# Attention with beacon keys and a multiplicative FFN on one Trainium2 core: part of the first loads moves to the second DMA queue as fp32, and the first x is transposed on TensorE

## The chip, the cores and the metric

One core of one Trainium2 chip. The metric is device time in microseconds (us) of one execution of the program; lower is better. The profile shows one execution; times inside it count from its first instruction, and its span runs from the first to the last instruction.

## The reference

Shapes: B = 8 batches, H = 8 heads, S = 576 rows, 16 beacon rows, D = 64; x has 4608 rows of 512; w1, w2 are 512x1024, w3 is 1024x1024, w_out is 1024x512. All inputs and the output are fp32.

```python
k_all = np.concatenate([beacon_k, k], axis=2)          # 592 keys
v_all = np.concatenate([beacon_v, v], axis=2)
scores = scale * np.matmul(q, k_all.transpose(0, 1, 3, 2))
scores = np.where(causal, -1e9, scores)                # beacon keys always visible
a = np.exp(scores - scores.max(-1, keepdims=True))
a /= a.sum(-1, keepdims=True) + 1e-09
attn = np.matmul(a, v_all)                             # (B, H, S, D)
x = attn.transpose(0, 2, 1, 3).reshape(B * S, H * D)   # 4608 x 512
out = ((x @ w1) * (x @ w2) @ w3) @ w_out
```

## The kernel before

Everything is computed in fp16 with fp32 sums. The order of the instructions on each engine is the order in which the code is written; nothing is rescheduled.

**Attention.** A batch is eight steps: four pairs of heads, each in two halves of the query rows. Step `s` belongs to batch `b = s // 8`, with `r = s % 8`. `scores(s)` makes transposed scores on TensorE (L300), `exps` the exponentials on ScalarE (L309), `mask` the causal products on VectorE (L321), `values(s)` the product with v, with a column of ones in v for the sums (L338), then the division on VectorE (L346, L347) into `x16`, row-major. The scores of step `s + 1` are written ahead of the values of step `s`. Scores need q and k with the head dimension on the partitions (`qT`, `kT`): for batch 0 TensorE transposes them (L194), for later batches a DMA does (`transpose_qk`, L123 and L124, ten per batch). After the last pair of heads of a batch five more transposing DMAs (L358) bring `x16` into `xT`, the form that the FFN needs.

**FFN.** Since nothing stands between `@ w3` and `@ w_out`, the kernel multiplies the two first (`fuse`: TensorE transposes of w3, L203, and 64 matmuls, L213, into `Wt`). Then come nine chunks of 512 rows: `ff_ab` (64 matmuls, L233, with w1 and w2 in `w12`) and `ff_out` (32 matmuls, L254; the results leave by L265). All of this is one stream, 64 + 9 x 96 matmuls; `emit_ff(n)` writes its next n matmuls. The table `fill[s]` says how many go into step `s`, and `n_first` how many more between batch 0 and batch 1. In the kernel before that is 16 in each of steps 4 to 7, then 60, then 36 over batch 1, then some 11 in each step; what is left is written at the end. Chunk 1 needs rows of batch 1, chunk 2 of batch 2, and so on.

**Queues.** Two queues issue DMAs. POOL's loads everything that comes from memory and casts fp32 to fp16 on the way (q L99, k and v L108 with their beacon rows L112, w_out L172, w3 L176, w1 and w2 L179). SP's does the transposing DMAs and the output. Each queue issues in the order of the code, and an entry that waits holds up those behind it. On each queue at most eight DMAs are under way: an entry also waits for the landing of the one eight places ahead. q, k, v and their transposed forms have two buffers each (`b % 2`), so a load waits until the batch that last used its buffer is through with it.

Of the kernel before, what the change touches and what calls it, by code (L numbers as in the profile page):

```python
# [39 lines left out]
def kernel(  # L40
# [13 lines left out]
    nc = tc.nc  # L54
# [70 lines left out]


    for i in range(NB2):
        nc.vector.memset(k16s[i][64:128, 4, :], 0.0)
        nc.vector.memset(vas[i][64:128, 4, :, :], 0.0)
# [9 lines left out]
    load_q(0, 0)  # L139
    load_k(0, 0)  # L140
    load_q(0, 1)
# [8 lines left out]
    )  # L150
    load_k(0, 1)
    for c in range(2, NJT):
        load_q(0, c)
        load_k(0, c)
    for m, base in (
# [14 lines left out]
    for c in range(NJT):  # L170
        load_v(0, c)
    nc.gpsimd.dma_start(wo16, moe_w_out.rearrange("(t p) n -> p t n", p=P))  # L172

    w316 = xT[:, :, ds(M // 2, 2 * DF)].rearrange("p a (c r) -> p a c r", c=2)
    for kt in range(NFT):
        nc.gpsimd.dma_start(w316[:, kt // 2, kt % 2], moe_w3[ts(kt, P), :])  # L176
# [12 lines left out]

    for c in range(NJT):  # L190
        pt = psM.tile([P, 2, NT, P], FP16, name="pm")
        for i, d16 in enumerate((q16s[0], k16s[0])):
            for t in range(NT):
                nc.tensor.transpose(pt[:, i, t, :], d16[:, c, ts(t, P)], ident)  # L194
        nc.vector.tensor_copy(qTs[0][:, :, ts(c, P)], pt[:, 0])
        nc.scalar.copy(kTs[0][:, :, ts(c, P)], pt[:, 1])


# [126 lines left out]
    def values(s):  # L325
# [41 lines left out]
    for s in range(4, 8):  # L367
        fill[s] = 16
    for s in range(NSB, 2 * NSB):
        fill[s] = (96 - n_first) * (s - NSB + 1) // NSB - (96 - n_first) * (s - NSB) // NSB  # L370
    rest, n = 6 * 96 - LEFT, NS - 2 * NSB
    for s in range(2 * NSB, NS):
# [71 lines left out]
```

## Time and profile before

| | |
|---|---|
| median of 3 runs | 347.77 us (347.2 to 348.11) |
| the profiled execution | 346.73 us, span 345.0 us |
| mean granted TensorE clock | 0.951 |
| busy: TensorE, VectorE, ScalarE, POOL | 293.3, 152.5, 153.4, 121.7 us |
| first scores of batch 0, of batch 1 | 14.51, 76.87 us |

A timeline row reads: start, duration, engine, line, operation, output<-inputs, shape, count, and in brackets the idle time of that engine ahead of it and what ended it. A row of DMA issues gives the count, the size of one as written, and the median time from issue to landing. GB/s counts the bytes written; a load that casts reads twice as many.

### The profile page before, as it was taken

What the parts mean: (1) busy time and instruction counts of PE and PEld (TensorE: products, weight loads), DVE (VectorE), ACT (ScalarE), POOL (GpSimd) and SP (SyncE); (2) the same over time, 40 slices, a digit from 0 to 9 for tenths busy, and PEclk for the clock granted to TensorE, in tenths of its full rate; (3) what the DMA queues carried; (4) which work ended last, traced back from release to release, by engine and by line L of the source; (5) the groups of instructions that cost most, each with busy time, mean ns of one, the idle gap of its engine ahead of it and who ended that gap; (6) DMA issues with size and microseconds to landing.
All of it is one profiled execution on the core that took longest, in us unless ns stands there. A gap on an engine that the chain in (4) does not pass through costs nothing.

```text
span 345.0 us, 6756 instructions
## 1 busy us (share of the span) xinstructions
PE 293.3 (85%) x2696; PEld 149.0 (43%) x2696; DVE 152.5 (44%) x363; ACT 153.4 (44%) x214; POOL 121.7 (35%) x162
## 2 busy tenths in 40 slices
PE   2686980897943999599999989999999999999995
PEld 1353540344421445245554544555545544444442
DVE  3253430145611555426565546556555555344342
ACT  2481430237620675146636745664666473031220
POOL 8944558658419400950096048214000000000000
PEclk9998997699966899879999999999999999999999
DMA  9999999999999991999299999999833203301103
GB/s 66 119 159 209 196 170 139 150 155 154 172 162 156 142 141 29 145 202 148 42 121 213 141 116 164 189 137 144 198 79 73 111 2 67 125 1 61 63 0 122
DMA packets 182447, 42.99 MB, mean 125 GB/s; under 512 B 171664, under 2 KB 176784, under 8 KB 182416
## 3 DMA queue, kind: packets, MB, share of 16 engines
q0 software_dynamic: 121232, 19.67, 84.7%
q1 hardware_dynamic: 61184, 22.89, 38.3%
q8 instruction: 21, 0.34, 0.4%
q14 instruction: 10, 0.08, 0.1%
HBM read 39.32 MB, written 9.44 MB: 141 GB/s over the span
## 4 chain that ended last, share of the span: by engine, by line
PE 60%; DMA 23%; POOL 8%; ACT 3%; issue 2%; DVE 2%; SPq 2%; POOLq 0%; DVEq 0%
PE pm L233 28%; PE pm L254 13%; PE pv L338 8%; DMA xT<-x 6%; PE ps L300 5%; DMA k<-in_k_dram 5%; DMA qT<-q 5%; PE pm L213 4%; DMA xT<-in_moe_w_dram 3%; DMA q<-in_q_dram 3%; POOL q L99 2%; POOL va L108 2%; POOL k L108 2%; ACT pT L309 2%; SPq L358 1%
## 5 line engine op out<-in xcount | busy, mean ns | idle before, releaser
L233 PE MATMUL pm<-xT,w 128*128 128x512 f16 x576 | 136.8, 390 | 19.8 <-DMA xT<-x 19.8
L309 ACT ACTIVATE pT<-ps 128x736 f16<-128x736 f32 (+3 forms) x128 | 106.3, 863 | 43.2 <-PE ps L300 42.5
L244 ACT ACTIVATE a_sb<-pm 128x512 f32<-128x512 f32 x72 | 43.0, 597 | 109.0 <-PE pm L233 107.8
L233 PEld LDWEIGHTS <-w 128*128 128x128 f16 x576 | 55.2, 100 | 83.6 <-issue 27.2
L246 DVE TENSOR_TENSOR gT<-pm,a_sb 128x512 f16<-128x512 f32 x72 | 49.7, 690 | 67.5 <-PE pm L233 67.2
L254 PE MATMUL pm<-Wt,gT 128*128 128x512 f16 x288 | 67.8, 383 | 0.0
L108 POOL DMA_DIRECT2D va<-in_v_dram x40 | 33.7, 861 | 80.4 <-PE pv L338 57.4
L300 PE MATMUL ps<-qT,kT 64*128 64x80 f16 (+3 forms) x704 | 39.7, 237 | 13.4 <-ACT pT L309 6.4
L338 PE MATMUL pv<-va,pT 128*128 128x65 f16 x960 | 43.3, 198 | 2.7 <-DVE pT L321 2.6
L346 DVE RECIPROCAL rd<-pv 128x4 f32<-128x4 f32 x64 | 12.1, 189 | 74.3 <-PE pv L338 74.3
L338 PEld LDWEIGHTS <-pT 128*128 128x128 f16 x960 | 35.1, 100 | 13.2 <-issue 4.9
L300 PEld LDWEIGHTS <-kT 64*128 64x128 f16 x704 | 21.7, 97 | 43.7 <-issue 39.3
L254 PEld LDWEIGHTS <-gT 128*128 128x128 f16 x288 | 26.9, 98 | 29.6 <-issue 0.8
L99 POOL DMA_DIRECT2D q<-in_q_dram x40 | 34.7, 869 | 12.6 <-DMA k<-in_k_dram 3.3
L108 POOL DMA_DIRECT2D k<-in_k_dram x40 | 34.4, 859 | 9.1 <-DMA q<-in_q_dram 6.1
L264 DVE TENSOR_SCALAR ot<-pm 128x512 f32<-128x512 f32 x36 | 24.8, 690 | 21.5 <-PE pm L254 21.0
L347 DVE TENSOR_TENSOR x<-pv,rd 128x256 f16<-128x256 f32 x64 | 31.4, 491 | 2.6
L321 DVE TENSOR_TENSOR pT<-pT,MB 128x512 f16<-128x512 f16 x64 | 19.1, 325 | 1.6 <-ACT pT L309 1.6
L213 PE MATMUL pm<-wo,wT 128*128 128x512 f16 x64 | 15.7, 392 | 0.0
L321 DVE TENSOR_TENSOR pT<-pT,MA 128x480 f16<-128x480 f16 x32 | 12.8, 399 | 2.8 <-ACT pT L309 2.8
L222 ACT CAST Wt<-pm 128x512 f16<-128x512 f32 x8 | 4.7, 586 | 16.7 <-PE pm L213 16.7
L205 DVE COPY wT<-pm 128x1024 f16<-128x1024 f16 x8 | 5.5, 689 | 8.4 <-PE pm L203 8.4
(29 smaller groups left out, 56.9 us busy)
## 6 DMA issues: line engine op xcount, KB each, us to landing
out_dram<-ot SPq DMA_DIRECT2D x36, 256.0 KB, 3.0
q<-in_q_dram POOLq DMA_DIRECT2D x32, 128.0 KB, 9.7
k<-in_k_dram POOLq DMA_DIRECT2D x24, 128.0 KB, 10.8
va<-in_v_dram POOLq DMA_DIRECT2D x24, 128.0 KB, 6.4
xT<-in_moe_w_dram POOLq DMA_DIRECT2D x8, 256.0 KB, 13.0
w<-in_moe_w_dram POOLq DMA_DIRECT2D x8, 256.0 KB, 10.1
wo<-in_moe_w_out_dram POOLq DMA_DIRECT2D x1, 1024.0 KB, 10.8
k<-in_k_dram POOLq DMA_DIRECT2D x8, 112.0 KB, 8.4
```

Source lines behind the costliest of these rows:

```text
L99: nc.gpsimd.dma_start(q16s[b % NB2][:rows, c, :].rearrange("s (h d) -> s h d", h=H), q[b, :, ds(c * P, rows), :].rearrange("h s d -> s h d"),)
L108: nc.gpsimd.dma_start(dst[ds(p0, rows)], src[b, :, ds(s0, rows), :].rearrange("h s d -> s h d"))
L213: nc.tensor.matmul(pm, wT[:, rt, :], wo16[:, rt, :], start=(rt == 0), stop=(rt == NFT - 1),)
L233: nc.tensor.matmul(pm, w12[:, kt, ds(i * DF + kf * P, P)], xT[:, kt, ds(mc * 512, 512)], start=(kt == 0), stop=(kt == NKT - 1),)
L244: nc.scalar.activation(a_sb, pm, AF.Copy, scale=GS)
L246: nc.vector.tensor_tensor(gT[:, kf, :], pm, a_sb, ALU.mult)
L254: nc.tensor.matmul(pm, gT[:, kf, ts(mt, P)], Wt[:, kf, :], start=(kf == 0), stop=(kf == NFT - 1),)
L300: nc.tensor.matmul(ps[:, hh, ds(col, n)], kT[ds(hh * 64, 64), t, ts(jt, P)], qT[ds(hh * 64, 64), t, ds(q0, n)],)
L309: nc.scalar.activation(pT[:, :, ds(GO[g], GW[g])], pss[s][j][:, :, 0 : GW[g]], AF.Exp, scale=scale)
L321: nc.vector.tensor_tensor(blk, blk, m.unsqueeze(1).to_broadcast([P, 2, n]), ALU.mult)
L338: nc.tensor.matmul(pv[:, 2 * n + hh, 0:65], pT[:, hh, ds(col, P)], va[:, jt, 2 * t + hh, 0:65], start=(jn == 0), stop=(jn == len(BLK[i]) - 1),
L347: nc.vector.tensor_tensor(x16[:, ds(tiles[0], ni), ds(t * P, P)].rearrange("p i (h d) -> p i h d", h=2), pv[:, 0 : 2 * ni, 0:64].rearrange ...
```

## The change

- The five chunks of k of batch 0 (and its beacon rows) load as fp32 on SP's queue into a staging pool `stg` of six buffers; VectorE casts each into `k16` ahead of its transposes.
- w_out (four pieces) and w1, w2 (eight pieces of 128 rows) also load as fp32 on SP's queue, through the same six buffers. `cast_piece` casts a piece and issues the load of the next. One cast on VectorE stands in each of steps 0 to 6; the other five alternate between VectorE and ScalarE after the values of step 7.
- x of batch 0 is transposed by TensorE (20 transposes, with five copies from PSUM by VectorE and ScalarE) in the midst of `fuse`, eight matmuls after the values of step 7; the five transposing DMAs of batch 0 go away.
- `fill`: 5 matmuls in each of steps 3 to 7; `n_first` becomes 44 and counts from the end of `fuse`; 36 in batch 1 as before; 16 more than before are left for the end.
- The loads of q and k for batch `b + 2` are written in batch `b`, after the v of `b + 1`; those of batch 2 ahead of the loop.
- `ptp` (exponentials) has two buffers and not three.

```diff
-    ptp = ctx.enter_context(tc.tile_pool(name="ptp", bufs=3))
+    ptp = ctx.enter_context(tc.tile_pool(name="ptp", bufs=2))
+    stg = ctx.enter_context(tc.tile_pool(name="stg", bufs=6))
...
+    kst = []
+    for jt in range(NJT):
+        st = stg.tile([P, 2 * DM], FP32, name="st")
...
+        nc.sync.dma_start(
+            sv[ds(p0, rows)], k[0, :, ds(s0, rows), :].rearrange("h s d -> s h d")
+        )
+        if jt == 0:
+            nc.sync.dma_start(sv[0:Nb], beacon_k[0].rearrange("h n d -> n h d"))
+        kst.append((st, p0 + rows))
...
-    nc.gpsimd.dma_start(wo16, moe_w_out.rearrange("(t p) n -> p t n", p=P))
...
-    for c in range(4):
-        for i, w in enumerate((moe_w1, moe_w2)):
-            nc.gpsimd.dma_start(
-                w12[:, :, ds(i * DF + c * 256, 256)],
-                w[:, ts(c, 256)].rearrange("(t p) f -> p t f", p=P),
-            )
...
     for c in range(NJT):
+        st, rows = kst[c]
+        nc.vector.tensor_copy(k16s[0][:rows, c, :], st[:rows, 0:DM])
         pt = psM.tile([P, 2, NT, P], FP16, name="pm")
...
+    wo_v = moe_w_out.rearrange("(a c p) n -> a p c n", p=P, c=2)
+    pieces = [(wo16[:, ds(2 * a, 2), :], wo_v[a]) for a in range(4)]
+    for kt in range(NKT):
+        for i, w in enumerate((moe_w1, moe_w2)):
+            pieces.append((w12[:, kt, ds(i * DF, DF)], w[ts(kt, P), :]))
+    queued = []
+
+    def cast_piece(engine):
+        dst, st = queued.pop(0)
+        if engine is nc.scalar:
+            nc.scalar.copy(dst, st)
+        else:
+            nc.vector.tensor_copy(dst, st)
+        if pieces:
+            queued.append(staged(*pieces.pop(0)))
+
+    for _ in range(6):
+        queued.append(staged(*pieces.pop(0)))
+
+    def x0_transposed(i):
+        pt = psM.tile([P, NT, P], FP16, name="pm")
+        n = QTN[i]
+        for t in range(NT):
+            nc.tensor.transpose(pt[:, t, 0:n], x16s[0][:n, i, ts(t, P)], ident[:n, :n])
+        dst = xT[:, :, ds(QT0[i], n)]
+        if i % 2:
+            nc.scalar.copy(dst, pt[:, :, 0:n])
+        else:
+            nc.vector.tensor_copy(dst, pt[:, :, 0:n])
...
-        if t == NT - 1:
+        if t == NT - 1 and b > 0:
             for i in tiles:
                 nc.sync.dma_start_transpose(
...
-    LEFT = 40
-    n_first = 60
+    LEFT = 56
+    n_first = 44
+    n_second = 36
...
-    for s in range(4, 8):
-        fill[s] = 16
+    for s in range(3, 8):
+        fill[s] = 5
...
+    for c in range(NJT):
+        load_q(2, c)
+        load_k(2, c)
     for s in range(NS):
...
             values(s)
-            emit_ff(n_first)
+            emit_ff(8)
+            for i in range(NJT):
+                x0_transposed(i)
+            while queued:
+                cast_piece(nc.vector)
+                if queued:
+                    cast_piece(nc.scalar)
+                emit_ff(8)
+            emit_ff(64 + n_first - emitted)
...
+        if b == 0:
+            cast_piece(nc.vector)
...
             if r == 0:
                 for c in range(NJT):
-                    load_q(b + 1, c)
-                    load_k(b + 1, c)
-                for c in range(NJT):
                     load_v(b + 1, c)
+                for c in range(NJT if b + 2 < B else 0):
+                    load_q(b + 2, c)
+                    load_k(b + 2, c)
```

Here, with `staged`, a load on SP's queue is issued into a fresh `st` buffer.

On SP's queue, from the end of batch 0 on, there stood before (`xT` is x transposed, `qT_69` and `kT_71` the buffers of odd batches, `qT_68` and `kT_70` those of even ones, here batch 2; `out_dram<-ot` is an output):

```order
L358 DMA_TRANSPOSE xT<-x_267 128x4x128 x3
L358 DMA_TRANSPOSE xT<-x_267 128x4x80
L123 DMA_TRANSPOSE qT_69<-q_1_63 128x4x128
...
L123 DMA_TRANSPOSE qT_68<-q_0_62 128x4x128
L124 DMA_TRANSPOSE kT_70<-k_0_64 128x4x128
L265 DMA out_dram<-ot 128x512
...
L123 DMA_TRANSPOSE qT_68<-q_0_62 128x4x64
```

and stand now, on the same queue:

```order
L212 DMA st<-in_moe_w_dram 128x1024 x8
L124 DMA_TRANSPOSE qT_69<-q_1_63 128x4x128
...
L124 DMA_TRANSPOSE qT_68<-q_0_62 128x4x64
L125 DMA_TRANSPOSE kT_70<-k_0_64 128x4x128
L406 DMA_TRANSPOSE xT<-x_888 128x4x112
L406 DMA_TRANSPOSE xT<-x_888 128x4x128
L313 DMA out_dram<-ot 128x512
```

The x transposes of batch 0 left the queue, the weight pieces came ahead of it, and all ten transposes for batch 2 now stand ahead of the first output; before, eight of the ten stood behind it.

On POOL's queue, from the first v of batch 0 on (`va` holds v, `xT<-in_moe_w` is w3, which is parked in a part of `xT`, `w_59` is w1 and w2), there stood before, ahead of batch 1's q:

```order
L108 DMA va_66<-in_v_dram 80x8x64
L172 DMA wo_61<-in_moe_w_out_dram 128x8x512
L176 DMA xT<-in_moe_w_dram 128x1024 x8
L179 DMA w_59<-in_moe_w_dram 128x4x256 x8
L99 DMA q_1_63<-in_q_dram 128x8x64
```

and now:

```order
L100 DMA q_0_62<-in_q_dram 64x8x64
...
L109 DMA va_66<-in_v_dram 112x8x64
...
L109 DMA va_66<-in_v_dram 80x8x64
L188 DMA xT<-in_moe_w_dram 128x1024 x8
L100 DMA q_1_63<-in_q_dram 128x8x64
```

The k of batch 0, w_out, w1 and w2 are gone from between. From batch 1's q on, the order of POOL's queue is the same in both kernels: q and k of batch 2, then v of batch 2, then q and k of batch 3 follow one another as they did, since POOL ran ahead of the loop already.

On VectorE, around step 7 in the kernel now (`w_59<-st` is the cast of a piece of w1 or w2, `xT<-pm` the copy of a transposed x):

```order
L394 RECIPROCAL rd<-pv 128x6
L395 TENSOR_TENSOR x_294<-pv,rd 128x3x128
L253 COPY wT<-pm 128x1024
L244 COPY xT<-pm 128x4x112
L244 COPY xT<-pm 128x4x128
L244 COPY xT<-pm 128x4x80
L227 CAST w_59<-st 128x1024
```

None of these copies of x and none of the casts stood on VectorE before.

More of the change, by code (lines that the diff above doesn't have):

```diff
@@ L124, in transpose_qk @@
         nc.sync.dma_start_transpose(kTs[i][:, :, ds(c * P, P)], k16s[i][:, c, :])
+    kst = []
+    for jt in range(NJT):
+        st = stg.tile([P, 2 * DM], FP32, name="st")
+        p0 = Nb if jt == 0 else 0
+        s0 = max(0, jt * P - Nb)
+        rows = min(P - p0, S - s0)
+        sv = st[:, 0:DM].rearrange("s (h d) -> s h d", h=H)
+        nc.sync.dma_start(
[4 more added lines that the diff above has]
+        kst.append((st, p0 + rows))
     for i in range(NB2):
@@ L139 @@
     load_q(0, 0)
-    load_k(0, 0)
     load_q(0, 1)
@@ L150 @@
     )
-    load_k(0, 1)
     for c in range(2, NJT):
         load_q(0, c)
-        load_k(0, c)
     for m, base in (
@@ L196, with staged @@
         nc.scalar.copy(kTs[0][:, :, ts(c, P)], pt[:, 1])
+    def staged(dst, src):
+        st = stg.tile([P, 2 * DM], FP32, name="st")
+        if len(src.shape) == 3:
+            nc.sync.dma_start(st.rearrange("p (c n) -> p c n", c=2), src)
+            return dst, st.rearrange("p (c n) -> p c n", c=2)
+        nc.sync.dma_start(st, src)
+        return dst, st
+    wo_v = moe_w_out.rearrange("(a c p) n -> a p c n", p=P, c=2)
[24 more added lines that the diff above has]
+            nc.vector.tensor_copy(dst, pt[:, :, 0:n])
     def fuse():
@@ L363 @@
     NS = B * NSB
-    LEFT = 40
-    n_first = 60
+    LEFT = 56
+    n_first = 44
+    n_second = 36
     fill = [0] * NS
-    for s in range(4, 8):
-        fill[s] = 16
+    for s in range(3, 8):
+        fill[s] = 5
     for s in range(NSB, 2 * NSB):
-        fill[s] = (96 - n_first) * (s - NSB + 1) // NSB - (96 - n_first) * (s - NSB) // NSB
-    rest, n = 6 * 96 - LEFT, NS - 2 * NSB
+        fill[s] = n_second * (s - NSB + 1) // NSB - n_second * (s - NSB) // NSB
+    rest, n = 7 * 96 - n_first - n_second - LEFT, NS - 2 * NSB
     for s in range(2 * NSB, NS):
```

## The prediction

> **What bounds the kernel now.** I read the page first: engine sums, slices, sums of the DMA queues.
>
> ```profile
> span 345.0 us, 6756 instructions
> PE 293.3 (85%) x2696; PEld 149.0 (43%) x2696; DVE 152.5 (44%) x363; ACT 153.4 (44%) x214; POOL 121.7 (35%) x162
> PEclk9998997699966899879999999999999999999999
> DMA  9999999999999991999299999999833203301103
> ```
>
> TensorE is the bound, but not evenly: its granted clock (PEclk) sinks near slices 7, 11 to 13 and 17, all in the first half, and DMA is busy there. So I asked for windows between TensorE's stalls (columns: busy time and count of each engine, clock, DMA share, GB/s).
>
> ```profile
> 0.00:14.51 14.51, 5.60 (x40) 3.67 (x41) 4.18 (x22) 3.33 (x5) 13.34 (x24) 1.00 1.43 91
> 25.82:50.72 24.90, 21.94 (x205) 12.80 (x204) 8.78 (x19) 8.49 (x13) 13.10 (x17) 0.93 1.43 194
> 50.72:61.58 10.86, 0.00 (x1) 0.03 (x1) 0.75 (x2) 0.00 (x0) 9.07 (x12) 0.74 2.20 143
> 76.87:94.12 17.25, 15.22 (x216) 8.21 (x215) 9.66 (x29) 13.09 (x17) 11.57 (x15) 1.00 2.34 163
> 94.12:110.21 16.09, 5.45 (x57) 2.84 (x58) 3.26 (x9) 2.86 (x4) 8.17 (x11) 0.69 1.73 154
> 146.11:345.00 198.89, 189.91 (x1684) 94.08 (x1683) 98.70 (x219) 93.64 (x132) 37.22 (x47) 0.99 0.93 110
> ```
>
> After 146.11 TensorE is 95% busy: little is to be had there. Before it, the timeline of TensorE names the stalls, and the chain of waits gives the price of 64 matmuls undisturbed.
>
> ```profile
> 14.51 0.92 PE L300 MATMUL ps<-qT,kT 64*128 64x128 f16 x8
> 28.46 0.94 PE L203 MATMUL pm<-ident,xT 128*128 128x128 f16 x8 [2.64 <-DMA xT<-in_moe_w_dram]
> 30.54 2.62 PE L213 MATMUL pm<-wo,wT 128*128 128x512 f16 x8
> 33.01 0.61 PE L203 MATMUL pm<-ident,xT 128*128 128x128 f16 x8
> 33.45 1.89 PE L213 MATMUL pm<-wo,wT 128*128 128x512 f16 x8
> 61.58 15.36 PE L233 MATMUL pm<-xT,w 128*128 128x512 f16 x60 [10.86 <-DMA xT<-x]
> 76.87 0.55 PE L300 MATMUL ps<-qT,kT 64*128 64x128 f16 x8
> 96.86 0.49 PE L300 MATMUL ps<-qT,kT 64*128 64x128 f16 x4 [2.75 <-DMA kT<-k]
> 99.70 0.61 PE L300 MATMUL ps<-qT,kT 64*128 64x256 f16 x4 [2.35 <-DMA qT<-q]
> 100.24 1.50 PE L338 MATMUL pv<-va,pT 128*128 128x65 f16 x24
> 101.55 2.30 PE L254 MATMUL pm<-Wt,gT 128*128 128x512 f16 x5
> 110.21 4.14 PE L233 MATMUL pm<-xT,w 128*128 128x512 f16 x10 [4.90 <-DMA xT<-x]
> 146.11 1.87 PE L233 MATMUL pm<-xT,w 128*128 128x512 f16 x4 [4.03 <-DMA xT<-x]
> 150.06 3.24 PE L233 MATMUL pm<-xT,w 128*128 128x512 f16 x11
> 201.98 0.40 PE L300 MATMUL ps<-qT,kT 64*128 64x256 f16 x4 [1.58 <-DMA qT<-q]
> 202.31 0.90 PE L338 MATMUL pv<-va,pT 128*128 128x65 f16 x24
> 299.48 13.81 PE pm L233 x64
> ```
>
> The brackets are the idle time. After the longer ones the matmuls run slow at first: 10 in 4.14 us at 110.21, where 64 in 13.81 us makes 0.216 each. So a stall costs its length and a slow restart.
>
> **The change, front part (to the scores of batch 1, now at 76.87).** What DMA could do there:
>
> ```profile
> DMA packets 12474, 1.57 MB, mean 92 GB/s; under 512 B 12474, under 2 KB 12474, under 8 KB 12474
> DMA packets 6835, 3.95 MB, mean 198 GB/s; under 512 B 1977, under 2 KB 6072, under 8 KB 6834
> 16.34 0.96 POOL L172 DMA_DIRECT2D wo<-in_moe_w_out_dram  x1
> 17.20 3.84 POOL L176 DMA_DIRECT2D xT<-in_moe_w_dram  x7
> L108 POOL DMA_DIRECT2D k<-in_k_dram x40 | 34.4, 859 | 9.1 <-DMA q<-in_q_dram 6.1
> xT<-in_moe_w_dram POOLq DMA_DIRECT2D x8, 256.0 KB, 13.0
> q<-in_q_dram POOLq DMA_DIRECT2D x32, 128.0 KB, 9.7
> out_dram<-ot SPq DMA_DIRECT2D x36, 256.0 KB, 3.0
> ```
>
> The first two are the windows 0 to 17 and 28 to 48 us. In the first, DMA moved 92 GB/s, with POOL busy issuing (13.34 of 14.51 us); in the second, with large rows, 198. So the weights cannot go faster than they did from 28 on, but can begin sooner, beside the small rows.
>
> (a) *k of batch 0.* POOL loses five issues of 0.859 and the beacon rows, 4.8 us; q ends that much sooner, k comes beside it. A load with small rows and no cast on SP's queue is not shown; its bounds are the 3.0 us of an output and the 9.7 of a loaded q. I take scores at 10.5 instead of 14.51: -4.0. But v of batch 0, now issued from 7 us, shares the engines with pieces of w_out; later by 0 to 6.7 us (9.7 less 3.0). I take 2, nearer to the low end, for the pieces under way are at most six. Net -2.0. The casts of k lie ahead of the transposes on VectorE, which waits there for TensorE anyway.
>
> (b) *w3.* Its first issue moves from 17.20 to 12, with no w_out of 1 MB ahead of it, and is first needed near 21 (step 3). The wait of 2.64 goes, with its slow restart: 2.62 - 1.89 and about 0.94 - 0.61 twice, 1.4. Net -4.1; bounds -4.1 and 0, if the pieces on SP slow w3 to its old time. I take the first, since w3 gains 5 us and w1, w2 come after it.
>
> (c) *x of batch 0.* The idle 10.86 goes, and the slow restart, 15.36 - 60 x 0.216 = 2.4. Added: 20 transposes at 0.61/8, 1.5 us, and some 0.5 for the copies, which alternate on two engines; 39 matmuls of the fusion cover the rest, and the eight ahead of them cover the division of step 7. Net -11.3.
>
> (d) *Casts and smaller fills.*
>
> ```profile
> L205 DVE COPY wT<-pm 128x1024 f16<-128x1024 f16 x8 | 5.5, 689 | 8.4 <-PE pm L203 8.4
> L264 DVE TENSOR_SCALAR ot<-pm 128x512 f32<-128x512 f32 x36 | 24.8, 690 | 21.5 <-PE pm L254 21.0
> ```
>
> A cast of 1024 fp32 costs between 0.69 (1024 fp16) and 1.38 us (twice 512 fp32). Seven lie in steps 0 to 6. VectorE is busy 9.66 of 17.25 us over the eight steps of batch 1, so 1.2 a step, beside steps of 2.2 us; a cast fits where its piece has landed. Bounds 0 and 9.7 (all seven exposed); the cover is nearest to full, and I take 1.5 us. If a piece is late, VectorE holds the division behind it and TensorE with that: what is late next is the landing of pieces 6 to 11.
>
> (e) Sixteen matmuls fewer before batch 1 and more at the end: -3.45 at the mark, 0 in the sum. `ptp`: the buffer now reused belongs to values two steps back, done by then: 0.
>
> Sum: -2.0 - 4.1 - 11.3 + 1.5 = -15.9; scores of batch 1 at 76.87 - 15.9 - 3.45 = 57.5.
>
> **The change, after that.** (f) *Start of batch 2.* SP's queue:
>
> ```profile
> 72.05 1.20 SPq L124 DMA_TRANSPOSE kT<-k  x1
> 85.91 0.36 SPq L265 DMA_DIRECT2D out_dram<-ot  x1
> ```
>
> The last eight transposes for batch 2 stood 14 us behind an output that was not computed yet. By the new order all ten stand ahead of the first output, so they run before batch 1 ends: -2.75 - 2.35, and the restart (1.50 - 0.90; 2.30 - 5 x 0.216): -6.9. This comes from x leaving SP's queue and from the later `ff_out`, not from loading two batches ahead: on POOL's queue the loads stand in the order they had. I cost that edit at 0.
>
> (g) *Chunk 1.* Before, it began right at batch 2; now 16 matmuls of chunk 0 remain, so 21 matmuls (4.5 us) and the scores and values of two steps (0.55 and some 0.6 each) lie between the last values of batch 1 and it, 6.8 us.
>
> ```profile
> 103.91 6.17 DMA xT<-x
> ```
>
> This is the last x that it needs; it landed at 110.08, 8.3 us after those values ended (101.74). So 1.5 us of idling stay: -4.90 - (4.14 - 2.16) + 1.5 = -5.4; bounds -6.9 and 0.
>
> (h) *Chunk 2* comes 16 matmuls later too, over 10 us after its x: -4.03, restart 1.87 - 0.86 and 3.24 - 2.38, and 0.6 for the values between, as at 100.24: -6.5.
>
> (i) The 1.58 at 201.98 (transposes for batch 5 behind outputs) I leave: outputs come later against the batch, loads too.
>
> Sum: -15.9 - 6.9 - 5.4 - 6.5 = -34.7. The profiled execution took 346.73, so 312.0; it stands 1.04 under the median of the runs, 347.77. Forecast: 313.
>
> [...] DMA at 198 GB/s, written in halves, from 28 to 48 us shows the engines loaded without a second queue. [...]
>
> **Rivals.**
> 1. *DMA stays the bound of the front.* For: 198 GB/s does not rise with a second queue; small rows may starve beside large ones. Then w1, w2 land near 48 as now and q, k of batch 1 behind them; the scores of batch 1 begin near 70: 313 + 12 = 325.
> 2. *Slower.* The casts on VectorE, in order, pace batch 0 by the landing of pieces, in two rounds of six buffers. With the median landing of w3, 13.0, two rounds end near 35 us and hide. With (f) to (h) kept, it turns slower when the scores of batch 1 come after 76.87 - 3.45 + 18.8 = 92, which needs the last piece at about 72 (some 20 us of matmuls follow it), rounds of 33 us. At 36 a round: 353. Against: that median.
> 3. *POOL held up by the casts.* The pieces are the first copies from SBUF to SBUF on VectorE, and no row shows what POOL does beside one. The five of k, 3.5 us at 0.69, lie where POOL issues v; if they hold it, 313 + 3.5 = 316, and with half the pieces' 13.8 besides, 323. [...]
> 4. *The change does not do what it says at batch 2*: q and k of batch 2 land late behind v of batch 1 and the transposes still end after batch 1: 313 + 7 = 320.
> 5. *All is covered*: v not late, chunk 1 not late, casts hidden: 313 - 2 - 1.5 - 1.5 - 1.6 = 306.
>
> **How the numbers follow.** Forecast 0.60 (own range 307 to 320), rival 1 0.15, 2 0.04, 3 0.07, 4 0.07, 5 0.07. The range 305 to 326 takes in all but rival 2 and the tails. About 0.3% of the time, 1 us, can be told from no change. Only rival 2 is slower; same needs it halfway, 0.02; faster 0.94.
>
> **What the new profile would show.** Right: no wait of L281 for `xT<-x` at the first chunk; first scores near 10.5 and those of batch 1 near 57; more GB/s before 17 us; no wait of scores for `qT` or `kT` at batch 2; chunk 1 waiting under 2 us, chunk 2 none; clock 0.9 or more in every slice from 25 us on. Wrong: TensorE idle in steps 0 to 7 behind the division or the mask with VectorE waiting for `st`; L251 waiting for w3 longer than 3 us; scores of batch 1 waiting for transposes whose q landed late; POOL's issues of v longer than 0.86.

## The result: 328.37 us, faster, but by 19 us and not by 35

| | before | after |
|---|---|---|
| median | 347.49 us (346.31 to 348.11, 4 runs) | 328.37 us (327.29 to 328.72, 4 runs) |
| profiled execution, its span | 346.73, 345.0 us | 327.29, 325.6 us |
| first scores of batch 0, of batch 1 | 14.51, 76.87 us | 18.23, 65.94 us |
| last v of batch 0 landed | 19.5 us | 26.6 us |
| chunk 1, chunk 2 begin | 110.21, 146.11 us | 99.08, 131.21 us |

The ratio is 0.9448 [0.9414, 0.9483]. The forecast was 313 us, 305 to 326, so the direction was right and the size wrong, by 15 us. Of k_sp and k1_sp, below, the profiled execution was a slow one (331.54 and 341.08 us), so the times given for these two are medians of their three other runs.

The page of the changed kernel, the lines that answer to those shown of before:

```profile
span 325.6 us, 6823 instructions
PE 288.3 (89%) x2716; PEld 148.4 (46%) x2716; DVE 162.1 (50%) x381; ACT 156.1 (48%) x218; POOL 111.3 (34%) x147
PEclk9999999999997999999999999999999999999999
DMA  9999999999999999999999999997741221301103
```

The clock now sinks in one slice only, at 98.9 us (0.50 for 3.41 us). The first slices are not to be read, since the digit stands at 9 before the trace has a record of the clock: 14 matmuls of scores take 0.83 us at 27.29 and 0.52 at 34.90, and the trace's first record of the clock, at full, begins at 34.0 us (21.8 before). Stretches of the same work as before: up to the first scores, batch 1, batch 2 up to chunk 1, and from chunk 2 to the end (columns as in the prediction).

```profile
0.00:18.23 18.23, 5.11 (x40) 3.86 (x41) 6.19 (x27) 3.63 (x5) 11.67 (x22) 1.00 1.26 195
65.94:85.55 19.61, 15.21 (x216) 8.21 (x215) 9.60 (x29) 14.00 (x19) 13.64 (x17) 1.00 2.05 144
85.55:99.08 13.53, 8.45 (x107) 4.39 (x106) 6.27 (x16) 5.37 (x7) 6.29 (x8) 0.99 1.85 146
131.21:325.60 194.39, 185.65 (x1633) 91.62 (x1631) 98.44 (x217) 91.38 (x130) 36.64 (x46) 1.00 0.97 113
```

In the first row DMA moves 195 GB/s where it moved 91, and yet the stretch is 3.7 us longer. Batch 1 has the same 216 matmuls as before and takes 19.61 us where it took 17.25. TensorE's timeline names the waits:

```profile
17.26 0.61 PE L202 MATMUL pm<-ident,q 128*128 128x128 f16 x4 [2.27 <-DMA q<-in_q_dram]
18.23 0.91 PE L348 MATMUL ps<-qT,kT 64*128 64x128 f16 x8
23.85 0.32 PE L386 MATMUL pv<-va,pT 128*128 128x65 f16 x3 [2.30 <-DMA va<-in_beacon_v_dram]
25.57 1.79 PE L386 MATMUL pv<-va,pT 128*128 128x65 f16 x24
56.35 9.66 PE L281 MATMUL pm<-xT,w 128*128 128x512 f16 x44
65.94 0.55 PE L348 MATMUL ps<-qT,kT 64*128 64x128 f16 x8
74.22 0.35 PE L348 MATMUL ps<-qT,kT 64*128 64x80 f16 x10 [1.11 <-ACT pT L357]
89.78 0.35 PE L348 MATMUL ps<-qT,kT 64*128 64x80 f16 x10 [1.17 <-DMA kT<-k]
99.08 2.74 PE L281 MATMUL pm<-xT,w 128*128 128x512 f16 x6 [3.87 <-DMA xT<-x]
131.21 2.32 PE L281 MATMUL pm<-xT,w 128*128 128x512 f16 x10
```

Before chunk 0 (56.35) and chunk 2 (131.21) there is no wait any more, where there were 10.86 and 4.03. The 4.90 before chunk 1 became 3.87. Two waits are new, both for the small rows of batch 0: 2.27 for the last q and 2.30 for v. The values of step 1 begin at 25.57, where they began at 19.30:

```profile
19.30 1.50 PE L338 MATMUL pv<-va,pT 128*128 128x65 f16 x24
```

The window of 6 to 12.5 us of the DMA issues says why, first before, then after:

```profile
va<-in_v_dram POOLq DMA_DIRECT2D x1, 112.0 KB, 3.3
```

```profile
va<-in_v_dram POOLq DMA_DIRECT2D x3, 128.0 KB, 16.0
q<-in_q_dram POOLq DMA_DIRECT2D x1, 64.0 KB, 11.9
```

POOL issues v sooner than before (from 6.98 us on), but a v takes 16.0 us to land where the first took 3.3 (and the others up to 4.4). So the two halves of the miss are: the scores of batch 1 came at 65.94 and not at 57.5 (8.4 us), and from there to the end the kernel gained 8.5 us (268.1 to 259.7) where the forecast had 15.4 (6.9 us).

### The profile page after: what moved, and what is told of

The parts are those of the page before. It is cut to its first block, busy times and chain, and to the rows that moved or that the text cites. A ratio compares the mean times of both kernels' runs of the same rounds, so it can differ in the third digit from the quotient of the medians.

```text
span 325.6 us, 6823 instructions
## 1 busy us (share of the span) xinstructions
PE 288.3 (89%) x2716; PEld 148.4 (46%) x2716; DVE 162.1 (50%) x381; ACT 156.1 (48%) x218; POOL 111.3 (34%) x147
## 4 chain that ended last, share of the span: by engine, by line
PE 64%; DMA 15%; ACT 5%; POOL 4%; SPq 4%; DVE 3%; issue 3%; POOLq 0%; DVEq 0%
PE pm L281 27%; PE pm L302 16%; PE pv L386 9%; PE ps L348 6%; DMA va<-in_v_dram 5%; PE pm L261 4%; ACT pT L357 4%; DMA xT<-x 3%; DMA qT<-q 3%; DMA k<-in_k_dram 3%; DMA kT<-k 3%; POOL q L100 2%; SPq L125 2%; SPq L124 2%; PE pm L251 1%
## 5 line engine op out<-in xcount | busy, mean ns | idle before, releaser
L281 PE MATMUL pm<-xT,w 128*128 128x512 f16 x576 | 133.0, 382 | 3.9 <-DMA xT<-x 3.9
L281 PEld LDWEIGHTS <-w 128*128 128x128 f16 x576 | 54.0, 98 | 64.2 <-DMA xT<-x 4.4
L294 DVE TENSOR_TENSOR gT<-pm,a_sb 128x512 f16<-128x512 f32 x72 | 49.7, 690 | 48.4 <-PE pm L281 47.9
L302 PE MATMUL pm<-Wt,gT 128*128 128x512 f16 x288 | 66.7, 379 | 0.0
L348 PEld LDWEIGHTS <-kT 64*128 64x128 f16 x704 | 21.8, 97 | 42.2 <-issue 38.2
L109 POOL DMA_DIRECT2D k<-in_k_dram x35 | 29.9, 853 | 18.5 <-DMA va<-in_v_dram 7.0
L202 PE MATMUL pm<-ident,q 128*128 128x128 f16 x20 | 3.0, 308 | 13.1 <-DMA q<-in_q_dram 13.1
L204 ACT COPY kT<-pm 128x512 f16<-128x512 f16 x5 | 2.9, 586 | 14.4 <-DVE qT L203 14.4
```

Source lines behind the costliest of these rows:

```text
L109: nc.gpsimd.dma_start(dst[ds(p0, rows)], src[b, :, ds(s0, rows), :].rearrange("h s d -> s h d"))
L281: nc.tensor.matmul(pm, w12[:, kt, ds(i * DF + kf * P, P)], xT[:, kt, ds(mc * 512, 512)], start=(kt == 0), stop=(kt == NKT - 1),)
L294: nc.vector.tensor_tensor(gT[:, kf, :], pm, a_sb, ALU.mult)
L302: nc.tensor.matmul(pm, gT[:, kf, ts(mt, P)], Wt[:, kf, :], start=(kf == 0), stop=(kf == NFT - 1),)
L348: nc.tensor.matmul(ps[:, hh, ds(col, n)], kT[ds(hh * 64, 64), t, ts(jt, P)], qT[ds(hh * 64, 64), t, ds(q0, n)],)
```

## Experiments

All ratios are to the kernel before, run beside. "Mark" is the start of the scores of batch 1.

### One: is x on TensorE worth its price?

```diff
 # before.py
-        if t == NT - 1:
+        if t == NT - 1 and b > 0:
...
+            for i in range(NJT):
+                x0_transposed(i)
             emit_ff(n_first)
```

> The kernel before with one part of the change: x of batch 0 goes through TensorE (20 transposes after the values of step 7) instead of five transposing DMAs; loads and fills as before. Theory (the wait for the first x is worth its length and its restart, and the next thing in its place is the transposes of q and k for batch 1): the idle 10.9 us before the first chunk shrinks under 2 us, no slow restart, scores of batch 1 near 66 instead of 76.9, time 335 to 339. Rival (SP's queue or DMA throughput up to then sets the scores of batch 1 anyway): the scores of batch 1 wait for qT or kT and come at 72 or later, time 342 or more.

339.76 us, 0.9779 [0.9716, 0.9842], 0.8 us above the range that was expected. TensorE's timeline:

```profile
53.77 13.11 PE L233 MATMUL pm<-xT,w 128*128 128x512 f16 x60 [0.53 <-ACT xT L369]
70.70 0.35 PE L300 MATMUL ps<-qT,kT 64*128 64x80 f16 x10 [2.12 <-DMA kT<-k]
93.58 0.61 PE L300 MATMUL ps<-qT,kT 64*128 64x256 f16 x4 [5.07 <-DMA qT<-q]
104.94 4.31 PE L233 MATMUL pm<-xT,w 128*128 128x512 f16 x11 [5.72 <-DMA xT<-x]
```

The 10.86 became 0.53 and the mark came at 66.81, 10.1 us sooner. That is nearly the mark of the full change, which has 16 matmuls fewer ahead of it (3.45 us): with loads and queues as before, the front is 2.6 us shorter than in the full change. Then waits at batches 1 and 2 and at chunk 1 eat part of the gain.

### Two: small rows behind the weights (held_q, held_v, rows_1k)

Three variants of the changed kernel. held_q lets the first six weight pieces go only when the last q of batch 0 has been transposed; held_v only when v of batch 0 has landed (by a memset on POOL behind its eight loads of w3); rows_1k cuts the same pieces into rows of 1 KB.

```diff
 # held_q (held_v: nc.gpsimd.memset, behind the issues of w3, casts from step 2 on)
         st = stg.tile([P, 2 * DM], FP32, name="st")
+        nc.vector.memset(st[:, 0:1], 0.0)      # the first six pieces only
 # rows_1k
-    wo_v = moe_w_out.rearrange("(a c p) n -> a p c n", p=P, c=2)
+    wo_v = moe_w_out.rearrange("(a c p) n -> a p c n", p=P, c=4)
+    # pieces of 256 columns: four rows of 1 KB a partition, w1 and w2 likewise
```

> The changed kernel, but the first six weight pieces on SP's queue wait until the last q of batch 0 is transposed (a one-column memset on VectorE before each load). Theory (the DMA engines take rows from the two queues in turn, so each 256-byte row of q or v waits for a 2 or 4 KB row of a weight): the last q lands near 13.5 instead of 17.2 and the first scores come near 14.5 instead of 18.2; v, which still meets the pieces, lands its last near 24 instead of 26.6. Rival 1 (casts on VectorE hold up what POOL writes): the casts of k are still there, so q lands near 17 as now. Rival 2 (small rows are limited among themselves, weights do not matter): q as now, 17; v as now, 26. Time by the theory 325 to 328, by the rivals 328 to 331.

> The changed kernel, but the first six weight pieces on SP's queue wait until v of batch 0 has landed (memsets on POOL behind the w3 loads); the fusion begins in step 4 with 6 matmuls a step, and the casts in step 2. Theory (rows in turn): the last v lands near 18 instead of 26.6 and the values of step 1 come near 19.5 instead of 25.6, since nothing large is ahead of them; w_out then meets w3 and lands between 24 and 33, so VectorE may wait for pieces from step 2 on and the total moves by less than the 6 us won: 322 to 330. Rival 1 (casts hold POOL) and rival 2 (small rows limit one another): v lands after 23 as now. What each says of the values of step 1 decides, not the total.

> The changed kernel with the same bytes in the same twelve pieces, but each piece cut so that its rows are 1 KB instead of 2 or 4 KB (step 3 has 4 and step 4 has 6 matmuls of the fusion, since the pieces are cut by columns). Theory (rows in turn, one for one): a row of v waits for 1 KB instead of 2 or 4, so v lands sooner while the pieces are under way (last v near 23 to 24 instead of 26.6), and w3 on POOL's queue gains on w1 and w2 (last w3 under 40 instead of 43.5). Rival (the queues share by bytes): v and w3 land as now. Time by the theory 325 to 328, by the rival 328 or, if short rows cost the engines more, 330.

held_q: 331.14 us, 0.9503 [0.9434, 0.9572]. The last q landed at 14.2 us and not at 17.2, and the first scores came at 16.11, where 14.5 had been expected. v took 7.9 us (window 6 to 12.5) and the last had landed at 18.0 us and not at 26.6, since the held pieces were issued from 16.7 us on and met it little (24 had been expected); the values of step 1 began at 20.89 and not at 25.57.

```profile
va<-in_v_dram POOLq DMA_DIRECT2D x3, 128.0 KB, 7.9
```

The time did not fall, since VectorE then stood at a cast of w_out whose piece landed late, with a mask for TensorE behind it. Its row on VectorE, and TensorE's:

```profile
24.81 0.69 DVE L229 CAST wo<-st 128x1024 f16<-128x1024 f32 x1 [3.78 <-DMA st<-in_moe_w_out_dram]
26.57 0.51 PE L388 MATMUL pv<-va,pT 128*128 128x65 f16 x6 [3.41 <-DVE pT L371]
```

held_v: 333.55 us, 0.9597 [0.9522, 0.9672], in the same manner: last v at 18.3, values of step 1 at 21.1, then 6.5 us at 26.6 behind a cast. Both times lie above what was expected (325 to 328 and 322 to 330). Both show that the weight pieces are what held v up, and neither is a cure.

rows_1k: 331.76 us, 0.9551 [0.9493, 0.9608]. The last v landed at 28.5, no sooner than with larger rows, against the expectation of 23 to 24. The first six pieces are 1280 rows in the changed kernel and 3072 here, fewer than the 4736 of v, so the last of v comes behind all six either way: the sixth landed at 23.6 and 26.9 us. What the run shows is how two queues share. Rows by queue (q0 is POOL's, q1 SP's) in the stretch in which both have work, of rows_1k (16 to 24 us):

```profile
q1 hardware_dynamic: 1961, 1.94, 88.2%
q0 software_dynamic: 1960, 0.25, 46.8%
```

and of the changed kernel (12 to 20 us), whose pieces have mostly rows of 2 KB there:

```profile
q1 hardware_dynamic: 1509, 2.32, 91.1%
q0 software_dynamic: 1520, 0.19, 36.2%
```

In these stretches, where both queues have work and large rows stand in one of them, as many rows of the one passed as of the other, to within 1%, with rows of 1 KB and of 2 KB. Where both bring rows of 256 bytes the counts differ (4278 by POOL's and 3178 by SP's in the changed kernel, 4 to 12 us), and no run says why. Beside each row of v, 256 bytes in memory, went one of 1 or 2 KB, so while the weights moved 2.32 MB in the changed kernel, v and its kind moved 0.19. In what order the rows of the two queues follow one another, these counts do not show.

### Three: k of batch 0 alone on the second queue (x_fill, k_sp)

x_fill is x_only with the smaller fills of the change; k_sp is x_fill with k of batch 0 as fp32 on SP, and no weight there.

```diff
 # x_fill, on x_only
-    LEFT = 40
-    n_first = 60
+    LEFT = 56
+    n_first = 44
+    n_second = 36
 # k_sp, on x_fill
-    load_k(0, 0)                      # and the four others, POOL
+        nc.sync.dma_start(sv[ds(p0, rows)], k[0, ...])      # fp32, five chunks
+        nc.vector.tensor_copy(k16s[0][:rows, c, :], st[:rows, 0:DM])
```

> The kernel before with x of batch 0 on PE and with the smaller fills of the change (44, 36, 56); all loads stay on POOL's queue in their old order, no casts on VectorE. Theory 1 (the DMA engines were full before, row by row, so the second queue gains nothing): first scores 14.5, scores of batch 1 at 63.4 or up to 3 us later where they wait for the transposes of q and k (the last landed at 68.6 in the run with x alone), no wait before chunk 2, total 324 to 330, that is, no slower than the full change at 328.4. Rival (the loads on the second queue carry part of the gain): slower than the full change by 3 us or more, 331 to 336, with the w3 wait of 2.6 and a long wait for q and k of batch 1.

> As x_fill, and k of batch 0 alone goes as fp32 on SP's queue with five casts on VectorE; no weight does. This is term (a) of the prediction by itself. Theory 1 (small rows pass the engines at about 0.95 thousand a microsecond whatever queue brings them): the 9344 rows of q and k still take 10 us, first scores between 13 and 16, last v landed at 17 to 19, values of step 1 at 18 to 20.5, total within 2 us of x_fill. Rival (the prediction: POOL's issuing was the limit): first scores at 10.5, last v 4 to 5 us sooner than the 19.5 of before, total 3 to 4 us under x_fill.

x_fill: 331.39 us, 0.951 [0.945, 0.9571], first scores at 14.77; its time lies at the edge of what the rival had (331 to 336). k_sp: 328.19 us, 0.9425 [0.9347, 0.9504], first scores at 16.26. By the medians it is 3.2 us under x_fill, as its rival had it, but the intervals overlap, so whether k_sp is faster is open; that its first scores are not sooner is not. They came at 15.94, 15.93 and 16.20 in the three later kernels with the same front (qk1_pe, x1_pe, both_pe). Rows that started between 4 and 12 us, in before, x_fill, k_sp and after, a fence each:

```profile
DMA packets 7827, 0.98 MB, mean 123 GB/s; under 512 B 7827, under 2 KB 7827, under 8 KB 7827
```

```profile
DMA packets 7781, 0.98 MB, mean 122 GB/s; under 512 B 7781, under 2 KB 7781, under 8 KB 7781
```

```profile
DMA packets 7578, 1.34 MB, mean 168 GB/s; under 512 B 7578, under 2 KB 7578, under 8 KB 7578
```

```profile
DMA packets 7456, 1.34 MB, mean 168 GB/s; under 512 B 7455, under 2 KB 7455, under 8 KB 7456
```

One queue or two, it is 930 to 980 rows a microsecond. That is the mean of this stretch and not a ceiling; with v alone, from 14 to 16 us in k_sp, it is 1,200, and no run says why it is lower at first:

```profile
DMA packets 2410, 0.30 MB, mean 152 GB/s; under 512 B 2408, under 2 KB 2410, under 8 KB 2410
```

The GB/s of k_sp and of the changed kernel are higher only because an fp32 row is written with 256 bytes and a cast one with 128. q and k of batch 0 are 9344 rows (8 heads of 576 and 592), some 10 us at that rate, and the last of them landed at 14.2 us in x_fill and at 14.4 in k_sp. The rival, that POOL's issuing was the limit there, is out for the first scores. They come later than in x_fill, with the rows landed at the same time, because of the casts. VectorE in k_sp:

```profile
14.82 0.42 DVE L210 COPY qT<-pm 128x512 f16<-128x512 f16 x1 [1.53 <-PE pm L209]
15.16 0.51 DVE L205 CAST k<-st 80x512 f16<-80x512 f32 x1
```

The last k had landed at 14.16, but its cast stands behind the copy of a transposed q and begins at 15.16. The rival keeps a part behind the first scores: with five issues fewer on POOL, w_out landed at 24.0 us and not at 27.7, and the last w at 44.8 and not at 48.5.

### Four: the fills (old_fill) and the order of loads (q1_early)

old_fill is the full change with the fills of before from chunk 0 on; q1_early is x_fill with q and k of batch 1 ahead of the second half of w1 and w2 on POOL.

```diff
 # old_fill, on after.py
-    LEFT = 56
-    n_first = 44
+    LEFT = 40
+    n_first = 60
 # q1_early, on x_fill
+    load_w12(0); load_w12(1)
     for c in range(NJT):
         load_q(1, c)
         load_k(1, c)
+    load_w12(2); load_w12(3)
```

> The full change with the fills of before (60 matmuls of chunk 0 ahead of batch 1, 36 in its steps, 40 left): tests terms (e) and (g). Theory (the steps of batch 1 became long because 20 of their 36 fill matmuls are ff_ab, whose ScalarE scaling stands in one queue with the exponentials): batch 1 takes 17 to 17.5 us instead of 19.6 and its scores begin at 69.4; chunk 1 then begins right at batch 2 and waits for x 6 to 9 us instead of 3.87, and chunk 2 waits again; total 330 to 334. Rival (the length of batch 1 has nothing to do with which matmuls fill it): it still takes 19.3 us or more.

> As x_fill, and on POOL's queue q and k of batch 1 stand ahead of the second half of w1 and w2 (columns that the first 44 matmuls of chunk 0 do not read). Theory 1 (loads are bound by the engines, so the order on one queue decides): q of batch 1 lands about 5 us sooner (46 to 53.5 instead of 51 to 58.4), its transposes end by 64, scores of batch 1 at 63 to 64 with no wait for kT in its steps, total 318 to 324, faster than the full change. Rival (the transposes are late for another reason, their own length of some 1.3 us each in a row, or the second half of w1, w2 is now late): scores of batch 1 no sooner than 65.9, or a wait for w of 2 us and more in the steps of batch 1, total 326 or more.

old_fill: 340.15 us, 0.9769 [0.9717, 0.9822], worse than the 330 to 334 that were expected. TensorE's timeline, then SP's:

```profile
69.26 0.55 PE L348 MATMUL ps<-qT,kT 64*128 64x128 f16 x8
88.17 0.33 PE L348 MATMUL ps<-qT,kT 64*128 64x128 f16 x4 [1.67 <-DMA kT<-k]
93.94 0.61 PE L348 MATMUL ps<-qT,kT 64*128 64x256 f16 x4 [5.43 <-DMA qT<-q]
103.40 4.67 PE L281 MATMUL pm<-xT,w 128*128 128x512 f16 x11 [4.05 <-DMA xT<-x]
```

```profile
68.22 1.19 SPq L125 DMA_TRANSPOSE kT<-k  x1
78.29 0.36 SPq L313 DMA_DIRECT2D out_dram<-ot  x1
78.74 1.26 SPq L124 DMA_TRANSPOSE qT<-q  x1
```

Batch 1 lasts from 69.26 to 86.50, where the wait of 1.67 begins: 17.24 us, where before took 17.25, with four `ff_ab` matmuls among its 36. The full change, with twenty, takes 19.61. That the kind of matmul decides was as expected; that it does so by the scaling of `a_sb` on ScalarE, ahead of the exponentials for which TensorE waits 1.11 at 74.22, is the likeliest way, and no run separates it. Not expected was that the transposes for batch 2 stand again behind an output, from 68.22 to 78.74, and 5.43 us of TensorE with them.

So with the old fills the new loads gain nothing over x alone (340.15 against 339.76), and with the new fills 331.39 against 328.37, intervals overlapping. The fills are worth 8.4 us with the old loads and 11.8 with the new.

q1_early: 330.09 us, 0.9484 [0.9421, 0.9547], like x_fill and as the rival had it; 318 to 324 had been expected. q of batch 1 landed 5 us sooner (51.6 for the last) but its last transpose at 67.5 (70.6 in x_fill), and TensorE still waited 2.40 in batch 1. The ten transposes are what is slow, 17.6 us from the first landing to the last (13.7 in x_fill).

### Five: fewer DMA transposes (qk1_pe, x1_pe), and one more load on SP (k1_sp, all_three)

All on k_sp. qk1_pe transposes q and k of batch 1 on TensorE, x1_pe x of batch 1; k1_sp loads k of batch 1 as fp32 on SP too, once POOL has issued w3; all_three is all of it.

```diff
 # qk1_pe
-                transpose_qk(1, c)
+                qk1_transposed(c)                  # 8 transposes, copies by VectorE and ScalarE
+                emit_ff(8 if c < NJT - 1 else n_first - 40)
 # x1_pe
-        if t == NT - 1 and b > 0:
+        if t == NT - 1 and b > 1:
...
+        if s == 2 * NSB:
+            for i in range(NJT):
+                x_transposed(1, i)
 # k1_sp
-        load_k(1, c)
+        if b == 0 and r >= 2:
+            nc.vector.tensor_copy(k16s[1][:rows, r - 2, :], st[:rows])   # loaded by SP
```

> k_sp with q and k of batch 1 transposed on PE (40 transposes, eight ahead of each eight matmuls of chunk 0) instead of ten DMA transposes. Theory (what is left of the miss in batch 1 is that q and k pass the DMA engines twice, the second time at 1.3 us a transpose): added 40 x 0.61/8 = 3.1 us on PE; gone are the wait of 2.35 for kT and its slow restart of about 3; scores of batch 1 at 65, batch 1 takes 19.5 to 20 us instead of 24.1, batch 2 at 84.5 to 85.5 instead of 86.1; total 327 to 329. Rival (q and k themselves land too late, not the transposes): PE waits 2 us and more for q or k ahead of the transposes, total 330 or more.

> k_sp with x of batch 1 transposed on PE too, in the first step of batch 2. Term (g) by itself: before chunk 1 PE waits 4.49 for the DMA transpose of x and restarts slowly for 3.4 us at half the clock (about 1.7 lost). Theory: both go, 20 transposes of 1.5 us and their copies come instead, total 4 to 5 us under k_sp, 324 to 325.5. Rival (the wait only moves: q and k of batch 2 or 3, or chunk 2's x, are late next): total within 2 us of k_sp's 329.

> k_sp with k of batch 1 also as fp32 on SP, issued when POOL has issued w3 (20 us), so beside w_out and w3; five casts in steps 2 to 6. Theory 1 (rows take turns on engines that are full): w_out, w3 and the last w land 2 to 4 us later than the 24.0, 34.1 and 44.8 of k_sp, q of batch 1 lands about as then (53.8 at the last, or 1 to 3 us sooner), total 327 to 331. Rival (POOL's issuing, 0.86 us a load, is the limit): q of batch 1 lands by 49.5, its transposes 4 us sooner, no wait for kT in batch 1, total 325 or less.

> qk1_pe, k1_sp and x1_pe together on k_sp. If the three remove waits that follow one another, 320 to 324, faster than the full change (328.4); if PE then waits for q and k of batch 2, whose DMA transposes landed at 84.9, or the loads of batch 2 and 3 set the pace, 325 to 329.

qk1_pe: 325.91 us, 0.9395 [0.9326, 0.9464]: scores of batch 1 at 62.12 and of batch 2 at 81.92, no wait for kT. x1_pe: 325.47 us, 0.936 [0.9303, 0.9416]: chunk 1 without a wait at 96.50, chunk 2 at 127.88. Both as expected or a little better.

k1_sp: 337.00 us, 0.9701 [0.9617, 0.9785], and all_three 338.09, 0.9728 [0.9674, 0.9782]: both far worse than either theory. VectorE and TensorE in k1_sp:

```profile
37.07 0.43 DVE L441 CAST k<-st 128x512 f16<-128x512 f32 x1 [11.80 <-DMA st<-in_beacon_k_dram]
38.56 0.51 PE L359 MATMUL pv<-va,pT 128*128 128x65 f16 x6 [11.23 <-DVE pT L342]
```

The small rows of k, now on SP, were issued from 25.0 us on and so beside POOL's w3, w1 and w2; they took 11.4 to 18.8 us to land. The cast for them stood on VectorE ahead of a mask, and TensorE lost 11.23 us (10.95 in all_three). Here the small rows were SP's and the larger ones POOL's, and it was the small ones again that came late, with as many rows of each: from 29 to 37 us of k1_sp, 1304 by POOL and 1307 of k by SP. The stall itself is rival 2 of the prediction, casts that pace batch 0 by late landings, in another kernel.

### Six: do the staged weights carry a gain of their own? (after_x1, both_pe)

after_x1 is the full change with x of batch 1 on TensorE, as in x1_pe; both_pe is qk1_pe and x1_pe together, so it has no weight on SP.

> The full change with x of batch 1 transposed on PE too: term (g) on the changed kernel itself. In it PE waits 3.87 for the DMA transpose of x before chunk 1 and then runs at half the clock for 3.4 us (1.7 lost). Theory: both go for 20 transposes (1.5 us) that the copies delay little, and the queue of DMA transposes of batch 2 and 3 is five shorter: 3 to 5 us under 328.4, 323.5 to 325.5. Rival (in the changed kernel the wait only moves to q and k of the next batches): 327 or more.

> k_sp (k of batch 0 on SP, every other load by POOL, no weight staged) with q and k of batch 1 and x of batch 1 transposed on PE. Theory (the weights' second queue and their casts bring nothing that the engines had free, so a version without them is at least as fast once the DMA transposes are out): scores of batch 1 at 62, batch 2 at 82, no wait before chunk 1, total 320 to 323.5, below after_x1. Rival (the staged weights carry a gain of their own): 325 or more, above after_x1.

after_x1: 329.29 us, 0.9486 [0.9449, 0.9523], no faster than the full change. both_pe: 322.80 us (321.79 to 326.01), 0.9306 [0.9269, 0.9343]: faster than the full change and than after_x1 beside it, with w_out, w1 and w2 loaded as before. Its time is as expected, its scores of batches 1 and 2 (64.23 and 84.03) came 2 us later than that. It is the fastest median here, though the interval overlaps that of x1_pe. Rows of TensorE's timeline, and windows of 3.41 us (as long as the clock stayed at 0.50 in after_x1), the first of the two in each kernel with the wait at batch 4 in it, of after_x1:

```profile
146.56 0.61 PE L348 MATMUL ps<-qT,kT 64*128 64x256 f16 x4 [2.29 <-DMA qT<-q]
142.95:146.37 3.42, 1.32 (x9) 0.41 (x7) 0.91 (x3) 2.00 (x3) 0.00 (x0) 1.00 1.69 133
146.37:149.78 3.41, 3.22 (x32) 2.02 (x33) 1.10 (x3) 0.00 (x0) 0.88 (x2) 0.50 0.66 107
```

and of both_pe, with its line of the granted clock:

```profile
95.05 1.46 PE L248 MATMUL pm<-xT,w 128*128 128x512 f16 x6
145.07 0.40 PE L315 MATMUL ps<-qT,kT 64*128 64x256 f16 x4 [2.71 <-DMA qT<-q]
140.66:144.08 3.42, 1.70 (x11) 0.58 (x9) 1.27 (x3) 2.00 (x3) 0.00 (x0) 1.00 1.69 154
144.08:147.49 3.41, 2.42 (x35) 1.53 (x36) 1.12 (x3) 0.07 (x1) 0.89 (x2) 1.00 1.11 139
PEclk9999999999999999999999999999999999999999
```

In after_x1 the 3.87 went and chunk 2 began at 127.58, 3.6 us sooner than in the full change; then waits of 2.29 at 146.56 and 1.82 at 207.37, each with 3.4 us at half the clock behind it, gave it back. So the rival was right for this kernel: the wait moved. In both_pe a longer wait, 2.71, cost no clock.

## Why the prediction was wrong

**The step that failed is the first reading.** From 92 GB/s up to 17 us against 198 later, the prediction concluded that the weights "can begin sooner, beside the small rows". GB/s was the wrong column: the line of DMA's busy share quoted ahead of it read 9 from the first slices on, and with 128 bytes written a row 978 rows a microsecond are 123 GB/s (the 92 have the idle first microseconds in them). That a second queue found no room is shown by what happened: it brought no more rows a microsecond (947 and 932), and the weights beside v delayed it by 7 us, which holding them back undid. This step carries 8.4 of the 15.4 us; the rest is in (e), (f) and (g). The prediction took POOL's issuing (13.34 of the first 14.51 us) for time that fewer issues would save; in k_sp five issues fewer brought the last q and k no sooner (14.4 us, 14.2 in x_fill), so most of that time was hidden behind the rows.

**(a)** k of batch 0: forecast -4.0 and v +2. k alone on SP gave first scores 1 to 1.5 us later (14.77 to 15.93 or 16.26): the casts of k on VectorE, put at nothing in the prediction, cost that. The weights behind it on the same queue moved v by 7 us (19.5 to 26.6). What they did to the first scores differs between executions: 18.23 in the changed kernel, 16.38 in old_fill with the same instructions up to there; the last v landed at 26.7 in old_fill too, and the values of step 1 began there at 25.69. At the values of step 1 the net is +6.3, not -2.0: the 8.3 us between these are the miss of the front. The bound for v, 0 to 6.7, came from 9.7, the median of q loads, none of which had weights on the other queue beside it; v's 16.0 lies outside it.

**(b)** The wait for w3 went, but not because w3 came sooner: its first piece landed at 27.8 us (28.4 before). The step that needs it came later. In k_sp, without weights beside it, the piece landed at 25.3.

**(c)** x on TensorE: forecast -11.3, x_only -10.1 at the mark. Right to 1.2 us.

**(d)** Casts: from the values of step 1 to the mark 40.4 us; before it was 57.6, and the forecast's terms (b), (c), (d) and (e) make 40.2 of that; the cover held. A cast of 1024 took 0.69 us, the lower bound. That the sums agree so closely is luck in part, since TensorE's matmuls were slow for longer than before (the 0.83 us at 27.29 against 0.52 at 34.90, with the first record of full clock at 34.0 us and not at 21.8), which the forecast did not have. The cover is thin: when pieces land later, TensorE waits 3.41 (held_q), 6.5 (held_v) and 11.23 us (k1_sp, where the pieces are k).

**(e)** "Sixteen matmuls fewer: 0 in the sum" left out that twenty of the 36 in batch 1 become `ff_ab`. Batch 1 lengthened by 2.36 us, and old_fill shows it at 17.24 with four.

**(f)** The two waits at batch 2, 5.10, became one of 1.17. Mechanism right, but x leaving SP's queue does not do it: old_fill, where it has left too, waits 1.67 and 5.43. The later `ff_out` is needed; no run has it without the other.

**(g)** Chunk 1: 3.87 left and not 1.5, since the last x that it needs landed 11.8 us after the values of batch 1 ended (87.27 to 99.03) and not 8.3, the landing time of before; and the slow restart stayed (six matmuls in 2.74 us, 1.4 more than at 0.216). (e), (f) and (g) miss 2.36 + 1.17 + 2.37 + 1.4 = 7.3 us; the second half of the miss is 6.9.

**(h), (i)** Chunk 2 without a wait, as forecast; the late wait for qT is 1.19 (1.58 before).

**The edit to two batches ahead** was costed at 0. No run tests it alone; the order of POOL's queue from batch 1 on is the same either way.

**The rivals.** Rival 1 is what happened, "small rows may starve beside large ones", with 325 as its time, and the last of w1 and w2 did land near 48 "as now" (47.2, and 48.4 before); it put the delay on q and k of batch 1, and it fell on q and v of batch 0. Its time is near by luck: its mark was 70, and the rest of the miss is (e) to (g). That "198 GB/s does not rise with a second queue" did not hold as written (28 to 40 us: 204 before, 284 after), but as read it did: 4.86 MB before (2.43 written, all cast) and 4.87 after (1.49 written with a cast by POOL, and 1.89 by SP as they were). Rival 4 came in part (1.17 of 5.10). Rival 3 came on a small scale: POOL issues a v in 862 ns on average, where it took 861 before; but two issues that a cast of a piece met took 1.20 us (37.90) and 1.24 (49.06), where the longest of a q, k or v took 1.02 before, and a cast that met an issue took 1.09 us (28.42) instead of 0.69. Not each meeting did this: the issue at 40.28 took 0.94 and the cast at 30.45 took 0.69. Together that is about 1 us. Rivals 2 and 5 did not come here. Of the signs named for "right", first scores at 10.5, the mark at 57, no wait for `kT` at batch 2, chunk 1 under 2 us and the clock in every slice failed; more GB/s before 17 us came true and meant nothing.

What stays open is how much the staged weights cost or gain by themselves with the new fills: x_fill and the full change differ by 3.0 us with overlapping intervals. That they are not needed, both_pe shows.

## What to carry to other kernels

Whether DMA has room is read from rows per microsecond and the busy share, not from GB/s: rows of 256 bytes kept the engines at a busy share of 9 with little over half the bytes of large ones (123 GB/s written against 198). A second queue brought no more rows there (7578 in 8 us by both, 7827 by one), and beside larger rows the small ones passed one for one (1520 to 1509), so what is needed first is better kept clear of larger rows: the last v landed at 18.0 us in held_q and at 26.6 in the changed kernel. A cast that stands ahead of other work on an engine makes all of it wait for the load: 11.80 us of VectorE and, behind it, 11.23 of TensorE in k1_sp. Before a gain is summed from waits that follow one another, ask of each what will be late next: here it was fifteen transposes by DMA, and without them k_sp's 328.19 us became 322.80.

## What was not expected of the hardware

- The row rate hardly changed with the queue or with the cast: from 4 to 12 us 7827 rows by POOL alone with casts (before), 7578 by both with 3064 of them uncast (k_sp).
- Where two queues had work and one of them large rows, they shared by rows: 1961 to 1960 (rows_1k, 16 to 24 us) and 1509 to 1520 (the changed kernel, 12 to 20 us).
- The clock fell after some short waits and not after others: it was 0.50 for 3.41 us after 2.29 (146.56, after_x1), and stayed at 1.00 after 2.71 (145.07, both_pe). In the traces of before and of the changed kernel every change of the clock lies a whole number of 3.41 us from the first record (21.78 and 34.01 us). Cut into such stretches from there on, these two traces have full clock give way to half after all seven stretches in which TensorE was idle for 2.31 us or more (half from 28.61, 55.92, 96.88, 107.12 and 144.66 us before, 98.86 and 324.14 after), and after none of the others, which have 1.78 at most. The wait of 2.29 fell nearly whole into one stretch (2.10 us idle there); that of 2.71 was split by a border (1.72 and 0.99).
- Full clock came back, in the same two traces, after the six of eleven stretches at half in which TensorE was idle for 0.32 us or less, and not after the five with 1.45 or more. So a wait of 2 to 3 us cost its length and either no clock (both_pe) or half of 3.41 us, 1.7 (after_x1), and more where the work behind it had gaps: after the 2.75 at batch 2 of before, with 2.35 behind it, the clock was 0.50 for 6.83 us (from 96.88).
